# S5 scan and multi-query attention on one core: two shift passes, scan sums in PSUM, matmuls in column parts, and a replanned order

## The chip, the cores and the metric

The kernel runs on one core of a Trainium2 chip. The metric is device time in microseconds of one execution, from the first to the last instruction of the core. The core's engines are TensorE (PE; its weight loads are listed as PEld), VectorE (DVE), ScalarE (ACT), GpSimd (POOL) and SyncE (SP), which issues most transfers. They run side by side and wait for each other with semaphores.

## The reference

Two independent layers, both over 2048 positions of 640 features, whose outputs are put side by side (2048 x 1280, bfloat16).

```
# A: diagonal state-space layer, 640 complex states
Lam_bar = exp(dt * Lam);  Bu = x @ B_bar.T
h[t] = Lam_bar * h[t-1] + Bu[t]                 # over 2048 positions
yA = 2 * real(h @ C.T) + x * Dskip
# B: attention, 32 query heads of 20, one key head and one value head
q = (x @ wq) in 32 heads;  k = x @ wk;  v = x @ wv
p = softmax(q k^T * 20**-0.5)                   # 32 heads x 2048 x 2048
yB = (p @ v, heads side by side) @ wo
```

## The kernel before, in words

**Attention.** Queries are cut into 4 blocks of 512 and heads into 8 groups of 4, which gives 32 groups; each has 4 heads x 16 key blocks of 128. A *tile* is one head's scores of 128 keys x 512 queries: 2048 tiles in all. A score matmul takes only 32 or 64 rows of PE's array (`fill_op`), so that two to four run side by side. The result goes to one of two score buffers in PSUM, R0 (three banks) and R1 (two banks), or for one tile to a bank B0 or B1, or to R0's third bank ("lent", key R0c).

The exponential of a tile is taken in one of two ways. *On ACT* (`ex_op`, line 1263): one activation over the two or three tiles of R0 or R1, written to P. *On DVE*: `dx_op` (line 1269) adds an offset to the scores and writes them as 16-bit integers, whose bits are read as bfloat16; that is a piecewise linear 2^x. To even out its error, three copies shifted by 33, 65 and 95 parts of 128 of an octave are made of it by `sh_op` (line 1274: subtract, clamp at zero), for up to three tiles at once, and each copy is weighted in the value matrix VP. Such a tile so needs four PV matmuls where one of ACT needs one. All PV matmuls (`pv_op`) take 32 of the array's columns each, one head per 32 columns, four side by side, and add up in the PSUM bank PV. At a group's end DVE copies PV out (`raw_op`, line 1307).

**Scan.** The complex recurrence is turned by a per-state angle into two real scans with a real decay. For each of 20 units (4 time blocks x 5 state blocks of 128): `scan_in` computes Bu's two parts on PE in B0 or B1, and DVE multiplies each with cosine and sine into tm0 to tm3 (line 901); `scan_unit` forms the two sums tm0 + tm3 and tm2 - tm1 on POOL, in four pieces each, into the buffer uh (line 917); DVE scans each (line 928) into hh; POOL multiplies back with cosine and sine (tm4 to tm7) and adds up to W (line 917 too). `y_tile` multiplies W with C on PE and DVE copies the result out (line 962).

**Background.** Other matmuls, of the full 128 x 128 array: scan inputs, y tiles, query projections (`qd_block`), output projections (`proj_ops`), and `zero` matmuls that only keep PE streaming. Each takes a bank B0 or B1 from its first matmul (`lock`) until DVE has copied the result (`free`).

**Order.** No engine chooses its order while it runs. While the program is built, `main` simulates the engines with a table of durations (`Plan.add`, `mm_t`, `dve_t`, `act_t`), at each step takes the candidate that could begin first, with biases, and appends it to its engine's list. `Plan.add` also books 0.106 us for PE when the kind of matmul changes, and the time slots in which a fast DVE pass and POOL would meet (`slot`). `vary` draws the biases anew for each of 64 turns from a number in SEEDS. `want_d` decides whether the next tile goes to DVE: up to QUOTA = 16 of 64 per group, when a bank is free and DVE's backlog is short. A PE operation is put off behind the next fill if it would end later than `t_fill[1]`, the time at which the R buffer is free plus a drawn allowance (`after`).

All instructions of PE are issued from one line (421).

Of the kernel before, what the change touches and what calls it, by code (L numbers as in the profile page):

```python
# [20 lines left out]
class Plan:  # L21
# [12 lines left out]
    PRE = dict(dve=0.135, pool=0.05)  # L34

    def __init__(self, nc):
# [12 lines left out]
        self.run = 0  # L49
        self.port = deque([(-1.0, 0.0)], maxlen=48)  # L50
# [159 lines left out]
def mm_t(n, cold=1.0):  # L210
    return n / 2400.0 * cold + 0.003
# [32 lines left out]
class _Kernel:  # L244
# [5 lines left out]
    SHIFTS = (0, 33, 65, 95)  # L250
# [14 lines left out]
    SEEDS = (19006, 20002, 21006, 22006, 23001, 24003, 25001, 26002, 27008, 28003, 0, 30006, 31008, 32005, 33006,  # L265
# [11 lines left out]

    def calibration(self):
# [3 lines left out]
        for i in range(n):  # L282
            for sh in self.SHIFTS:
                f = (i / n - sh / 128.0) % 1.0
                tot += 0.25 * (1.0 + f) * 2.0 ** -f
# [8 lines left out]
    def alloc(self):  # L294
# [68 lines left out]
        self.sb("uh", [128, 2, 512], BF16)  # L363
# [47 lines left out]

    def mms(self, lst, reads, writes, accum=False, kind="D", **k):

        occ = sum(mm_t(x[2].free_size()) / x[6] for x in lst)
# [15 lines left out]
    def setup(self):  # L430
# [102 lines left out]
        def copy(eng, tb):  # L533
            bt, off, key = banks[tb]
            for h in range(2):
                dst, src = K.KT[:, h, 512 * tb:512 * tb + 512], bt[:, off:off + 512]
                if eng == "act":
                    yield Op("act", lambda e, dst=dst, src=src, h=h: e.activation(  # L538
                        dst, src, ACT.Copy, scale=K.half[:, h:h + 1]), [key, "half"], [f"KT{h}_{tb}"], occ=act_t(512),
# [16 lines left out]
        for tb in range(2):  # L556
# [19 lines left out]
            *(Op("dve", lambda e, i=i, sh=sh: e.memset(K.VP[:, i, :, 20:21], 2.0 ** (sh / 128.0)), ["VP"], ["VP"], occ=dve_t(16))  # L576
              for i, sh in enumerate(self.SHIFTS)),
            *(Op("dve", lambda e, i=i, sh=sh: e.tensor_scalar(K.VP[:, i, :, 0:20], vps, 2.0 ** (sh / 128.0), None,
# [4 lines left out]
        for c in range(NC):  # L583
            pool(lambda e, c=c: e.tensor_copy(K.wqd[:, c, :].rearrange("p (d h) -> p d h", h=32),
                                              K.wq_raw[:, c, :].rearrange("p (h d) -> p d h", d=20)),
                 ["wq_raw"] + pk, [f"wqd{c}"], occ=1.6)
# [153 lines left out]
    def qt_block(self, qb, gg, hold=None, gate=None, done=None):  # L740
# [7 lines left out]
        def mm(c):  # L748
            return self.mms([self.m1(lambda: h.T[:, :], (K.wq1, K.wq0p)[gg == 0][:, c, :], K.xbT[:, c, 512 * qb:512 * qb + 512],
                                     c == 0, False)], ["ystage", f"xbT{c}"] if gg == 0 else ["wq1"] + xs, [None], accum=c > 0,  # L750
# [6 lines left out]
                     accum=True, hold=h),  # L757
# [4 lines left out]
    def qd_block(self, qb):  # L762
# [5 lines left out]
        for m in range(NC):  # L768
            h = Hold()
            for c in range(NC):  # L770
                ops.append(self.mms([self.m1(lambda h=h: h.T[:, :], K.wqd[:, c, 128 * m:128 * m + 128],
                                             K.xbT[:, c, 512 * qb:512 * qb + 512], c == 0, c == NC - 1)],
                                    [f"wqd{c}"] + xs, [None], accum=c > 0, lock=c == 0, gate=gate if c == 0 else None,
# [15 lines left out]
        for x in seq:  # L789
# [5 lines left out]
            else:  # L795
                ops.append(self.mms([self.m1(lambda: h.T[0:32, :], K.Md[:, ng, :], K.Qab[:, ng % 2, :].bitcast(BF16),
                                             ng == 0, ng == NC - 1, (0, 0))], ["Md", f"Qa{ng % 2}"], [None], accum=ng > 0,
# [19 lines left out]
    def scan_ops(self):  # L817
# [34 lines left out]
        for c in range(NC):  # L852
            cr, ci = K.Craw[c][:, 0, :], K.Craw[c][:, 1, :]
            keys = [f"Craw{c}0", f"Craw{c}1", "sc"] + (["ostage0", "ostage1"] if c == 4 else ws)
            for (dst, x, y, gx, gy, op, nm) in ((K.CGre, cr, ci, GRE, GIM, ALU.subtract, "CGre"),
                                                (K.CGim, ci, cr, NGRE, NGIM, ALU.add, "CGim")):
                for i in range(0, 640, 128):
                    pool(lambda e, y=y, c=c, gy=gy, i=i: e.tensor_scalar(K.ctmp[:, i:i + 128], y[:, i:i + 128], sc[:, gy, c:c + 1],  # L858
                                                                         None, op0=ALU.mult), keys, [f"ct{i}"] + ct * (i == 0), 128)
# [4 lines left out]
        for b in range(4):  # L864
            for c in range(NC):
                self.scan_in(sa, mk(sa, "dve"), b, c)
                self.scan_unit(mk(su, "dve"), mk(su, "pool"), mk(sr, "pool"), b, c)
# [21 lines left out]
    def scan_in(self, ops, dve, b, c):  # L889
# [4 lines left out]
        for k, (nm, BT) in enumerate((("BTre", K.BTre), ("BTim", K.BTim))):  # L894
            h = Hold()
            for cd in range(NC):
                ops.append(self.mms([self.m1(lambda h=h: h.T[:, :], BT[:, cd, 128 * c:128 * c + 128],
                                             K.xaT[:, b % 2, cd, :], cd == 0, cd == NC - 1)],
                                    [f"{nm}{i}" for i in range(NC)] + xs, [None], accum=cd > 0, lock=cd == 0,
# [7 lines left out]
    def scan_unit(self, dve, pool, back, b, c):  # L907
# [16 lines left out]
        after = lambda: prog["r"] >= u  # L924
        dec = bass.AP(tensor=K.sc, offset=self.RDEC * NC + c, ap=[[24 * NC, 128], [0, 512]])
        for ri in range(2):
            ini = 0.0 if b == 0 else K.hini[:, ri, c:c + 1]
            dve(lambda e, ri=ri, ini=ini: e.tensor_tensor_scan(K.hh[:, ri, :], dec, K.uh[:, ri, :], ini, ALU.mult,  # L928
                                                               ALU.add), ["sc", *(f"uh{ri}{h}" for h in self.PIECES), "hini"], [f"hh{ri}"],
                1100,  # L930
                gate=after, done=(lambda: prog.update(s=u + 1)) if ri else None)
# [11 lines left out]
    def y_tile(self, ops, dve, b, q):  # L943
# [3 lines left out]
        for h, (o0, o1, ds) in enumerate(((0, 384, (0, 1, 2)), (384, 640, (3, 4)))):  # L947
# [10 lines left out]
            for i in range(0, len(lst), self.YMM):  # L958
                ops.append(self.mms(lst[i:i + self.YMM], self.w_keys + ["CGre", "CGim", "DiagD"]
                                    + [f"xaT{b % 2}_{c}" for c in range(NC)], [None], accum=i > 0, lock=i == 0,  # L960
# [56 lines left out]
    def norm_last(self, g):  # L1017
# [4 lines left out]
                                 t == 0, t == 3) for t in range(4)], ["E1", f"OTr{sl}"], [None], lock=True, hold=h0)]  # L1022
# [16 lines left out]
    def proj_ops(self, qb, part=False):  # L1039
# [4 lines left out]
        for ts in ((2, 3) if part else range(4)):  # L1044
# [3 lines left out]
            for h in range(2):  # L1048
# [4 lines left out]
                for i in range(0, len(lst), self.PMM):  # L1053
                    ops.append(self.mms(lst[i:i + self.PMM], ots + wo, [None], accum=i > 0, lock=i == 0, hold=hd,
# [13 lines left out]
    def last_ops(self, gates, normed):  # L1068
# [6 lines left out]
        def mm(ts, k, begin):  # L1075
            if k < NC:
                src, rd, ok = K.OTd[:, k, :], [f"OTd{k}{self.PIECES[ts]}"], lambda: self.NQB - 1 in self.dense
            else:
# [3 lines left out]
                            rd + self.wo_keys, keys[ts], accum=not begin, gate=lambda: gates[ts]() and ok())  # L1082
# [448 lines left out]
```

## Time and profile before

| | us |
|---|---|
| median of 3 runs | 768.98 (768.0 to 770.19) |
| profiled execution: span | 768.6 |
| ACT busy | 752.5 |
| DVE busy | 708.3 |
| PE covered by matmuls | 704.8 |
| POOL busy | 446.0 |
| mean granted TensorE clock | 0.989 |

A row of the groups of instructions has: line, engine, operation, output<-input by the program's names, their shapes, count, then busy us and the mean length of one in ns, then the idle us of the engine just before them and what ended most of it. Busy time counts overlaps once. Two neighbours on DVE or ACT overlap in the record, since the next begins while the last one's result is still being written; a mean length is therefore more than the step from one to the next. A row of a tile has minimum, median and maximum in ns, the first and last start, and its forms. A row of the timeline has the start, the length and the instruction, with neighbours of one kind merged. A row of the waits has who waited, for whom, us in total, how often, and the longest. A window's row has the busy time of PE, PEld, DVE, ACT and POOL, each with its count, then the granted clock, the share of the DMA engines, and GB/s.

### The profile page before, as it was taken

Reading aid. Unit: us, or ns where it says so; the run is one execution under the profiler, and the core shown is the slowest. Engines: PE = TensorE matmul, PEld = TensorE weight load, DVE = VectorE, ACT = ScalarE, POOL = GpSimd, SP = SyncE. Lnnn points to the kernel's source line nnn. Section 1 sums busy time; section 2 is a strip of 40 time slices with the busy share of each in tenths; the row PEclk is TensorE's granted clock in tenths of the full one; section 3 lists DMA queues with packets and bytes.
Section 4 is the critical chain, followed back from the end, with each engine's and each line's share of the span. In section 5 each row is a group of like instructions: output and inputs, shape, how many; then the busy total and the mean of one; then the engine's idle time right before and its main releaser. Section 6 shows DMA issues by size and latency. Waiting matters only on the chain.

```text
span 768.6 us, 16664 instructions
## 1 busy us (share of the span) xinstructions
PE 704.8 (92%) x6538; PEld 213.4 (28%) x6538; DVE 708.3 (92%) x1236; ACT 752.5 (98%) x710; POOL 446.0 (58%) x867
## 2 busy tenths in 40 slices
PE   5799988888889999998889999988889999889998
PEld 2222222222222333322223323322223332223333
DVE  5599999999998999999997999999999789999986
ACT  8999999999999999999999999999999999999995
POOL 5612354579989931088997300199986469990040
PEclk9899999899999999999999999999999999999999
DMA  9366301000021100220002100040000201000020
GB/s 186 57 143 134 74 16 49 8 24 14 3 51 30 42 8 27 56 60 15 15 9 67 42 23 9 23 93 10 15 15 28 66 33 34 14 15 17 18 61 35
DMA packets 61179, 31.50 MB, mean 41 GB/s; under 512 B 41510, under 2 KB 61102, under 8 KB 61102
## 3 DMA queue, kind: packets, MB, share of 16 engines
q1 hardware_dynamic: 59606, 30.14, 15.9%
q8 instruction: 52, 0.85, 0.5%
q10 hardware_dynamic: 1496, 0.30, 0.2%
q14 instruction: 25, 0.20, 0.1%
HBM read 9.21 MB, written 12.69 MB: 28 GB/s over the span
## 4 chain that ended last, share of the span: by engine, by line
ACT 74%; PE 15%; DVE 9%; POOL 1%; DMA 1%; issue 1%; ACTq 0%; DVEq 0%; POOLq 0%
ACT P L1263 72%; PE R L421 5%; PE PV L421 5%; PE B L421 4%; DVE Pd L1274 4%; DVE Pd L1269 3%; DVE hh L928 1%; DVE tm L901 1%; POOL tm L858 1%; DMA WO<-in_B_wk_dram 1%; ACT cs L691 1%; ACT Pd L690 0%; ACT KT L538 0%; DVE CGre L860 0%; ACT L503 0%
## 5 line engine op out<-in xcount | busy, mean ns | idle before, releaser
L1263 ACT ACTIVATE P<-R 128x1024 bf16<-128x1024 f32 (+1 forms) x677 | 733.1, 1354 | 4.3 <-PE R L421 1.8
L421 PE MATMUL R<-QT,KT 32*128 32x512 bf16 (+1 forms) x1685 | 266.9, 389 | 48.6 <-ACT P L1263 37.1
L1269 DVE TENSOR_SCALAR Pd<-B 128x512 int16<-128x512 f32 x363 | 245.5, 682 | 19.4 <-PE B L421 17.0
L1274 DVE TENSOR_SCALAR Pd<-Pd 128x1536 int16<-128x1536 int16 (+2 forms) x513 | 260.2, 541 | 0.4
L421 PE MATMUL PV<-Pd,VP 128*32 128x512 bf16 x1744 | 256.9, 386 | 2.0 <-DVE OTr L1307 1.0
L421 PE MATMUL PV<-P,VP 128*32 128x512 bf16 x1612 | 253.3, 389 | 0.7 <-DVE OTr L1307 0.6
L917 POOL TENSOR_TENSOR tm<-hh,cs 128x128 bf16<-128x128 f32 x320 | 163.9, 533 | 17.7 <-DVE hh L928 8.3
L421 PEld LDWEIGHTS R<-QT,KT 32*128 32x128 bf16 (+1 forms) x1685 | 66.1, 91 | 301.0 <-ACT P L1263 271.0
L421 PE MATMUL B<-QT,KT 32*128 32x512 bf16 x363 | 141.0, 389 | 0.0
L917 POOL TENSOR_TENSOR uh<-tm 128x128 bf16<-128x128 bf16 x160 | 81.0, 527 | 97.6 <-DVE tm L901 93.7
L917 POOL TENSOR_TENSOR W<-tm 128x128 bf16<-128x128 bf16 x160 | 93.5, 608 | 49.4 <-PE B L421 45.3
L421 PEld LDWEIGHTS PV<-Pd,VP 128*32 128x32 bf16 x1744 | 60.1, 94 | 65.7 <-issue 40.5
L421 PEld LDWEIGHTS PV<-P,VP 128*32 128x32 bf16 x1612 | 58.1, 94 | 58.8 <-issue 46.6
L1011 POOL TENSOR_TENSOR OTd<-OTd,rwide 128x128 bf16<-128x128 bf16 x80 | 33.2, 443 | 60.0 <-DMA OTd<-o_rows 58.2
L1269 DVE TENSOR_SCALAR Pd<-R 128x512 int16<-128x512 f32 x73 | 49.9, 683 | 3.0 <-PE R L421 2.4
L901 DVE TENSOR_TENSOR tm<-B,cs 128x1024 bf16<-128x1024 f32 x40 | 48.5, 1213 | 1.0 <-PE B L421 0.6
L858 POOL TENSOR_SCALAR tm<-W,sc 128x128 f32<-128x128 bf16 x40 | 32.3, 821 | 27.5 <-DVE CGre L860 15.9
L421 PE MATMUL B<-CGre,W 128*128 128x384 bf16 (+1 forms) x160 | 46.4, 305 | 0.0
L421 PE MATMUL B<-CGim,W 128*128 128x384 bf16 (+1 forms) x160 | 45.5, 299 | 0.0
L928 DVE TENSOR_TENSOR_SCAN hh<-sc,hini,uh 128x512 f32<-128x512 f32 x30 | 40.7, 1358 | 0.0
L421 PEld LDWEIGHTS B<-QT,KT 32*128 32x128 bf16 x363 | 32.9, 91 | 0.0
L421 PE MATMUL B<-xaT,BTre 128*128 128x512 bf16 x100 | 30.1, 384 | 0.1
(149 smaller groups left out, 437.2 us busy)
## 6 DMA issues: line engine op xcount, KB each, us to landing
o_rows<-OTr SPq DMA_DIRECT2D x32, 128.0 KB, 1.7
QT<-q_rows SPq DMA_DIRECT2D x30, 128.0 KB, 2.2
q_rows<-Qd SPq DMA_DIRECT2D x16, 160.0 KB, 2.9
OTd<-o_rows SPq DMA_DIRECT2D x16, 160.0 KB, 3.4
out_dram<-ystage SPq DMA_DIRECT2D x16, 160.0 KB, 1.9
out_dram<-ostage SPq DMA_DIRECT2D x12, 160.0 KB, 1.8
P<-in_B_wq_dram SPq DMA_DIRECT2D x1, 800.0 KB, 5.6
WO<-in_B_wo_dram SPq DMA_DIRECT2D x4, 200.0 KB, 3.4
```

Of the source, the lines that this page charges most:

```text
L421: ins = e.matmul(o() if callable(o) else o, lhsT=l, rhs=r, start=st, stop=sp, skip_group_check=True, **kw)
L691: act(lambda e, c=c, b=b: e.activation(K.cs[:, c, :, :].rearrange("p i n -> p (i n)"), K.tri[:, 4 * b + 2:4 * b + 4, :].rearrange("p r n - ...
L858: pool(lambda e, y=y, c=c, gy=gy, i=i: e.tensor_scalar(K.ctmp[:, i:i + 128], y[:, i:i + 128], sc[:, gy, c:c + 1], None, op0=ALU.mult), key ...
L901: dve(lambda e, k=k, h=h: e.tensor_tensor(K.tm[:, 2 * k:2 * k + 2, :], bass.AP(tensor=K.BB, offset=512 * int(h.key[1]), ap=[[512 * self.BA ...
L917: put(lambda e, c0=c0, end=end: e.tensor_tensor(out[:, c0:end], a[:, c0:end], b[:, c0:end], op), reads, [writes + h], n, gate=None if i el ...
L928: dve(lambda e, ri=ri, ini=ini: e.tensor_tensor_scan(K.hh[:, ri, :], dec, K.uh[:, ri, :], ini, ALU.mult, ALU.add), ["sc", *(f"uh{ri}{h}" f ...
L1011: ops.append(Op("pool", lambda e, c=c, m=m: e.tensor_tensor(K.OTd[:, m, c], K.OTd[:, m, c], K.rwide[:, c], ALU.mult), rw + [f"OTe{dd}" for ...
L1263: return Op("act", lambda e: e.activation(dst, K.R[n % 2][:, 0:512 * size], ACT.Exp, scale=self.exp_scale), [f"R{n % 2}"] + ["R0c"] * (siz ...
L1269: return Op("dve", lambda e: e.tensor_scalar(K.Pd[:, 0, u, :], K.B[x][:, :], self.d_off, 0.0, op0=ALU.add, op1=ALU.max), [key], [f"Pd{u}_0 ...
L1274: return Op("dve", lambda e: e.tensor_scalar(K.Pd[:, i, a:b, :], K.Pd[:, 0, a:b, :], float(self.SHIFTS[i]), 0.0, op0=ALU.subtract, op1=ALU ...
```

## The change

1. *Shift passes.* The shifts become 0, 32, 64, 96. `sh_op` takes a pair (i, n) from PASSES = ((1, 1), (2, 2)): the first pass makes copy 1 from copy 0, the second makes copies 2 and 3 from copies 0 and 1 in one instruction over two separate slabs. The weights in VP are rounded to a bfloat16 value. A group closes at `self.shift` tiles, drawn as 3, 3 or 4.
2. *Scan sums.* uh is gone. PE adds tm0 and tm3 in a bank B with two matmuls against the identity; tm2 - tm1 with the identity and its negative (`nident`, one POOL operation in setup). The scan reads the bank and frees it.
3. *Column parts.* Background matmuls have kind C; `mms` cuts each of kind C or zero into four of 32 columns (`cols`), issued one after another.
4. *Planner.* A change of tiling costs 0.1 us, and only between the forms QK, D and C (PV, zero and C are one form); the exponentials overlap by AHEAD, TRAIL and GRAIN; some durations are new; a fill's due time is counted back from the end of the exponentials that are planned ahead of it; the draws have new ranges and new parameters (among them the quota of 16, 18 or 22), and SEEDS is new.

```diff
-    SHIFTS = (0, 33, 65, 95)
+    SHIFTS = (0, 32, 64, 96)
+    PASSES = ((1, 1), (2, 2))
...
+    @staticmethod
+    def form(kind):
+        return kind if kind in ("QK", "D", None) else "C"
...
         if eng == "pe":
-            occ += 0.106 if kind != self.pe_kind else 0.01
+            occ += 0.1 if self.form(kind) != self.form(self.pe_kind) else 0.01
...
         if eng == "dve":
-            lat += self.DRAIN
-        if kind == "fast" or eng == "pool":
+            lat = self.DRAIN
+        if kind == "ex":
+            start = max(start, self.exp_end - self.AHEAD)
+            self.exp_end = max(start + occ + self.TRAIL, self.exp_end + occ + self.GRAIN)
+            lat = self.exp_end - start - occ
...
+    def cols(lst):
+        def part(o, j):
+            return (lambda: o()[32 * j:32 * j + 32]) if callable(o) else o[32 * j:32 * j + 32]
+        return [(part(o, j), l[:, 32 * j:32 * j + 32], r, st, sp, (0, 32 * j), 4)
+                for o, l, r, st, sp, tp, _ in lst for j in range(4)]
...
     def mms(self, lst, reads, writes, accum=False, kind="D", **k):
+        if kind in ("C", "zero") and lst[0][5] is None:
+            lst = self.cols(lst)
...
-        pieces(pool, K.uh[:, 0, :], tm[0], tm[3], ALU.add, ["tm0", "tm3"], "uh0",
-               gate=lambda: prog["a"] > u and prog["s"] >= u)
-        pieces(pool, K.uh[:, 1, :], tm[2], tm[1], ALU.subtract, ["tm1", "tm2"], "uh1",
-               done=lambda: prog.update(u=u + 1))
...
+        for ri, (x, y, sign) in enumerate(((0, 3, K.ident), (2, 1, K.nident))):
             ini = 0.0 if b == 0 else K.hini[:, ri, c:c + 1]
-            dve(lambda e, ri=ri, ini=ini: e.tensor_tensor_scan(K.hh[:, ri, :], dec, K.uh[:, ri, :], ini, ALU.mult,
+            h = Hold()
+            unit.append(self.mms([self.m1(lambda h=h: h.T[:, :], w[:, :], tm[k], i == 0, i == 1)
+                                  for i, (w, k) in enumerate(((K.ident, x), (sign, y)))],
+                                 ["ident", "nident", f"tm{x}", f"tm{y}"], [None], kind="C", lock=True, gate=gate, hold=h,
+                                 done=(lambda: prog.update(u=u + 1)) if ri else None))
+            dve(lambda e, ri=ri, ini=ini, h=h: e.tensor_tensor_scan(K.hh[:, ri, :], dec, h.T[:, :], ini, ALU.mult, ALU.add),
+                ["sc", None, "hini"], [f"hh{ri}"], 1100, hold=h, free=True,
...
-        self.backlog = r.choice((2.5, 3.0, 3.5, 4.0, 5.0))
+        self.backlog = r.choice((2.0, 2.5, 3.0))
...
-        self.after = r.choice((0.1, 0.15, 0.2)), r.choice((0.35, 0.4, 0.5))
+        self.after = (r.choice((-0.1, 0.0, 0.1)),) * 2
...
+        self.alone, self.eager = r.choice((0.0, 0.1, 0.2, 0.4)), r.choice((0.1, 0.2, 0.3))
+        self.patience, self.shift = r.choice((0.0, 0.15, 0.3, 0.6)), r.choice((3, 3, 4))
+        self.quota, self.pvb = r.choice((16, 18, 22)), r.choice(((0.0, 0.6), (0.0, 0.3), (0.05, 0.5), (0.1, 0.6)))
...
-        def sh_op(us, i):
+        def sh_op(us, ps):
             a, b = us[0][0], us[-1][0] + 1
...
+            i, n = ps
+            return Op("dve", lambda e: e.tensor_scalar(K.Pd[:, i:i + n, a:b, :].rearrange("p s u n -> p s (u n)"),
+                                                       K.Pd[:, 0:n, a:b, :].rearrange("p s u n -> p s (u n)"),
+                                                       float(self.SHIFTS[i]), 0.0, op0=ALU.subtract, op1=ALU.max),
...
+                      occ=dve_t(512 * n * (b - a), 4), kind="fast")
...
-                    t_fill = (t_fill, t_fill + self.after[n % 2])
+                    due_t = p.exp_end + sum(act_t(512 * len(x)) + p.GRAIN for _, x in tiles) - p.TRAIL - 0.45
+                    t_fill = (t_fill, max(t_fill + 0.05, due_t - self.after[n % 2]))
```

More of the change, by code (lines that the diff above doesn't have):

```diff
@@ L34 @@
     PRE = dict(dve=0.135, pool=0.05)
+    AHEAD, TRAIL, GRAIN = 0.42, 0.115, 0.0133
     def __init__(self, nc):
@@ L959, in y_tile @@
                 ops.append(self.mms(lst[i:i + self.YMM], self.w_keys + ["CGre", "CGim", "DiagD"]
-                                    + [f"xaT{b % 2}_{c}" for c in range(NC)], [None], accum=i > 0, lock=i == 0,
+                                    + [f"xaT{b % 2}_{c}" for c in range(NC)], [None], accum=i > 0, kind="C", lock=i == 0,
                                     gate=gate if i == 0 else None, hold=hd))
@@ L1224, in d_group @@
                 g += 1
-            return g if g < NG and g in qt_done and sum(dcount[g]) < self.QUOTA else None
+            return g if g < NG and g in qt_done and sum(dcount[g]) < self.quota else None
         def t_left():
@@ L1317, in main @@
             if half and not any(x[1][0] == half[0][1][0] for x in dunits) and taken[half[0][1][0]] > self.DLAST:
-                shifts.extend((tuple(half), i) for i in range(1, 4))
+                shifts.extend((tuple(half), x) for x in self.PASSES)
                 half.clear()
@@ L1344, in main @@
                         if d:
-                            offer("fill", fill_op(n, [], d, bank(None)), 0.2, arg=([], d, bank(None)))
+                            offer("fill", fill_op(n, [], d, bank(None)), self.alone, arg=([], d, bank(None)))
             full = bool(tiles) and tile_left.get(tiles[0][0] - self.PTILES, 0) > 0
@@ L1362, in main @@
                 if n > 0 and n < 99:
-                    offer("pv", pv_op(g), 0.1 if n > self.few or whole or p.pe_kind == "PV" else 0.6)
+                    offer("pv", pv_op(g), self.pvb[not (n > self.few or whole or p.form(p.pe_kind) == "C")])
                 elif n == 0 and (full or dunit_left.get(cur["d"] - self.DUNITS, 0)) and any(items[g]):
@@ L1410, in main @@
             if kind == "flush":
-                shifts.extend((tuple(half), i) for i in range(1, 4))
+                shifts.extend((tuple(half), x) for x in self.PASSES)
                 half.clear()
@@ L1460, in main @@
                 if half and (u == 0 or half[0][1][0] != g):
-                    shifts.extend((tuple(half), i) for i in range(1, 4))
+                    shifts.extend((tuple(half), x) for x in self.PASSES)
                     half.clear()
```

89 lines of the change are left out of this document (47 added, 42 removed), and 8 rows, old and new, of the table SEEDS.

## The prediction

> **What bounds the kernel now.** I read the page's busy shares first, then the groups of instructions by form, then the stage between setup and tail as one window, then the waits.
>
> ```profile
> span 768.6 us, 16664 instructions
> ...
> PE 704.8 (92%) x6538; PEld 213.4 (28%) x6538; DVE 708.3 (92%) x1236; ACT 752.5 (98%) x710; POOL 446.0 (58%) x867
> ```
>
> ```profile
> 21.68 2.37 ACT L1263 ACTIVATE P<-R 128x1536 bf16<-128x1536 f32 x2
> ...
> 628.31 130.73 ACT L1263 ACTIVATE P<-R 128x1536 bf16<-128x1536 f32 x119 [0.28 <-PE B L421]
> 763.92 0.70 ACT L1101 ACTIVATE W<-R 128x640 bf16<-128x640 f32 x1 [4.88 <-PE R L421]
> ```
>
> ```profile
> 60.00:740.00 680.00, 632.52 (x5900) 188.18 (x5899) 645.59 (x1102) 677.27 (x627) 411.93 (x783) 0.99 0.13 33
> ```
>
> Three stretches: setup until the first exponential at 21.7, exponentials until 628.31 + 130.73 = 759.0, and a tail of 9.6 us. Between 60 and 740 ACT idles 2.7 us of 680, DVE 34.4, and PE is covered 93%. So in the middle the time is ACT's work, and it shrinks only if ACT gets less to do, or if setup and tail shrink.
>
> ```profile
> L1263 ACT ACTIVATE P<-R 128x1024 bf16<-128x1024 f32 (+1 forms) x677 | 733.1, 1354 | 4.3 <-PE R L421 1.8
> ```
>
> ```profile
> L1263 ACT ACTIVATE P<-R 128x1024 bf16<-128x1024 f32 x419 | 457.8, 1189 | 1.1 <-PE R L421 0.7 <-PE B L421 0.2
> L1263 ACT ACTIVATE P<-R 128x1536 bf16<-128x1536 f32 x258 | 418.3, 1621 | 3.2 <-PE R L421 1.2 <-PE B L421 1.1 <-PE PV L421 0.6
> ...
> L1269 DVE TENSOR_SCALAR Pd<-B 128x512 int16<-128x512 f32 x363 | 245.5, 682 | 19.4 <-PE B L421 17.0
> ...
> L1269 DVE TENSOR_SCALAR Pd<-R 128x512 int16<-128x512 f32 x73 | 49.9, 683 | 3.0 <-PE R L421 2.4
> ```
>
> The work is 2048 score tiles (32 head groups x 4 x 16). ACT takes 419 x 2 + 258 x 3 = 1612 of them, DVE 363 + 73 = 436. Together, overlaps counted once, they take 733.1 us (the page's row), so one tile costs ACT 0.455 us. **The exchange rate** between the two engines is what the change turns on: DVE time that is freed becomes time saved only by way of more tiles on DVE.
>
> **The change, part by part.** *Two shift passes instead of three.*
>
> ```profile
> L1274 DVE TENSOR_SCALAR Pd<-Pd x513: 272/550/840, 36.2 to 758.3; 128x1536 int16<-128x1536 int16 x118, 128x1024 int16<-128x1024 int16 x29, 128x512 int16<-128x512 int16 x24
> ```
>
> ```profile
> L1274 DVE TENSOR_SCALAR Pd<-Pd 128x1536 int16<-128x1536 int16 x354 | 205.5, 608 | 0.2
> ...
> L1274 DVE TENSOR_SCALAR Pd<-Pd 128x1024 int16<-128x1024 int16 x87 | 35.8, 450 | 0.2
> ...
> L1274 DVE TENSOR_SCALAR Pd<-Pd 128x512 int16<-128x512 int16 x72 | 20.9, 323 | 0.1
> ```
>
> ```profile
> 307.35 1.28 DVE L1269 TENSOR_SCALAR Pd<-B 128x512 int16<-128x512 f32 x2
> ...
> 310.08 1.96 DVE L1274 TENSOR_SCALAR Pd<-Pd 128x1536 int16<-128x1536 int16 x4
> ```
>
> There are 118 + 29 + 24 = 171 groups with three passes each. The elements stay the same (the second new pass does twice as many), so only the fixed part of 171 passes goes. Four passes of 1536 in 1.96 us follow each other at (1.96 - 0.08)/4 = 0.47 us, where 0.08 is what two neighbours overlap (two L1269 take 1.28, one takes 0.68, so they start 0.60 apart). The undisturbed lengths, 0.272 for one tile and 0.55 for three, give 0.139 a tile, so the fixed part of a 0.47 step is about 0.06: 171 x 0.06 = 10 us. By the means of the forms (323, 450, 608) it is 0.18 - 0.08 = 0.10, or 17 us, disturbances included. I take 10 and count the disturbances below.
>
> The second pass reads what the first wrote, which none of the old passes 2 and 3 did:
>
> ```profile
> 496.42 0.42 DVE L1274 TENSOR_SCALAR Pd<-Pd 128x1024 int16<-128x1024 int16 x1
> 496.75 0.68 DVE L1269 TENSOR_SCALAR Pd<-B 128x512 int16<-128x512 f32 x1
> 497.47 0.56 DVE L1274 TENSOR_SCALAR Pd<-Pd 128x1536 int16<-128x1536 int16 x1
> ```
>
> A pass that directly follows the L1269 that it reads starts 0.72 us after it instead of 0.60: 0.12 of waiting. At worst 171 x 0.12 = 20.5 us, at best nothing, when another DVE operation is put between; what waits behind it is DVE's whole queue. The old first pass had the same wait, and its groups show only 0.5 us of idle, so it is mostly covered; I take a loss of a third, 7.
>
> *Scan sums on PE.*
>
> ```profile
> L917 POOL TENSOR_TENSOR uh<-tm x160: 417/428/1295, 64.9 to 672.9; 128x128 bf16<-128x128 bf16 x160
> L928 DVE TENSOR_TENSOR_SCAN hh<-sc,hini,uh x30: 1267/1316/1546, 259.9 to 677.7; 128x512 f32<-128x512 f32 x30
> L928 DVE TENSOR_TENSOR_SCAN hh<-sc,uh x10: 1198/1258/1443, 72.6 to 234.1; 128x512 f32<-128x512 f32 x10
> ```
>
> ```profile
> L917 POOL TENSOR_TENSOR uh<-tm 128x128 bf16<-128x128 bf16 x160 | 81.0, 527 | 97.6 <-DVE tm L901 93.7
> ...
> L860 DVE SCALAR_TENSOR_TENSOR CGre<-W,sc,tm 128x640 bf16<-128x640 bf16 x4 | 3.5, 876 | 0.5 <-POOL tm L858 0.5
> ...
> L1104 DVE TENSOR_TENSOR W<-B,wqd 128x640 bf16<-128x640 f32 x1 | 0.8, 825 | 0.0
> ```
>
> POOL loses 81.0 of 446.0 us; it bounds nothing, so that alone is worth zero. But the spread of L1274 (0.55 median undisturbed, 0.608 mean) is 354 x 0.058 + some 5 for the small forms = 26 us of DVE waiting, which I put down to POOL's accesses. With 18% of POOL gone that is 5 us; with a third fewer passes too, up to 12; at least 0. The scans themselves fall from their medians towards their minima if they too stop colliding, 40 x 0.05 = 2 us (0 to 3.6 by the means): an operand in PSUM is no dearer in the two 640-wide rows, 825 against 876. The Trainium skill ("GPSIMD Engine Reference", section "Key points") says that GpSimd shares its SBUF interfaces with VectorE and contends with VectorE instructions in a two-port mode or with two SBUF inputs; the old scan has two SBUF inputs and the new one has one, so by that page the scans' gain would be the whole 3.6.
>
> PE gains 40 sums of two 512-column rounds, and each holds one of two banks until its scan ends, some 0.6 + 1.3 us, 76 us of 2 x 680. A sum waits at the head of PE's queue for DVE's L901; behind it stand the next fill and, for that, ACT.
>
> *Column parts.*
>
> ```profile
> 300.59 0.39 PE L421 MATMUL R<-QT,KT 32*128 32x512 bf16 x2
> ...
> 300.91 0.40 PE L421 MATMUL PV<-Pd,VP 128*32 128x512 bf16 x3
> ...
> 301.14 0.38 PE L421 MATMUL PV<-Pd,VP 128*32 128x512 bf16 x2
> ...
> 761.74 0.41 PE L421 MATMUL B<-ident,rden 128*32 128x128 bf16 x16
> ```
>
> ```profile
> PEld R L421 <- ACT P L1263: 271.0, 598, 1.5
> ...
> PEld B L421 <- issue: 59.9, 242, 0.4
> ...
> DVE Pd L1269 <- PE B L421: 17.0, 58, 0.7
> ```
>
> ```profile
> L421 PE MATMUL B<-xaT,BTre 128*128 128x512 bf16 x100 | 30.1, 384 | 0.1
> ...
> L421 PEld LDWEIGHTS PV<-P,VP 128*32 128x32 bf16 x1612 | 58.1, 94 | 58.8 <-issue 46.6
> ...
> L421 PEld LDWEIGHTS B<-xaT,BTre 128*128 128x128 bf16 x100 | 6.7, 97 | 13.7 <-issue 10.8 <-DVE Pd L1269 0.9 <-DVE Pd L1274 0.4
> ```
>
> A round of four PV matmuls takes 0.22 us (300.91 to 301.14), a fill followed by PV 0.32: a change of tiling costs PE 0.10. 242 loads for B waited so; those that came from PV and not from a fill are saved, with as many on the way back: 0 to 24 us, I take 15. The 40 sums cost 40 x 2 x 0.22 = 17. PE's work stays about even, hidden behind its 271 us of waiting for ACT. What it wins is order: sums, projections and PV share one tiling and can be mixed. The four parts are paid in instructions (roughly 900 matmuls become 3600), which run at the same rate: 16 small ones of 128 columns, four abreast, end 0.41 after the first began, 0.05 a round beside the 0.2 that a single one takes. The Trainium skill ("TensorEngine Tiling (Array Packing)", section "Restrictions and Gotchas") speaks against this part: column tiling switches Fast Weight Load off. By it each of the four loads could cost what one costs now; the trace has 94 ns for a 32-column load beside 97 for a 128-column one, but four of them vanish behind every 0.22 us round.
>
> *Planner.* DVE idles 34.4 us between 60 and 740, 17.0 + 2.4 of the whole run behind a late PE. The quota of DVE tiles per group rises from 16 to 16, 18 or 22, fills need not go first any more, and durations change. I take 15 of this idle time as filled; bounds -10 (banks held by scans, fills crowding) and +25. Setup gets one short POOL operation, hidden behind 320 us of POOL idling; no DMA is added or moved. The tail saves some four changes of tiling, 0.4.
>
> **Sum.** DVE time freed F = 10 - 7 + 5 + 2 + 15 = 25 us; bounds 10 - 20.5 + 0 + 0 - 10 = -20 and 17 + 0 + 12 + 3.6 + 25 = 58 (the 17 counts some disturbance twice). A further tile costs DVE 0.60 + (0.47 + 0.87)/3 + 0.05 = 1.10 us. Moving n tiles shortens the run by 0.455 n, in which DVE loses as much: F = 1.10 n + 0.455 n, n = F/1.555. F = 25 gives 16 tiles and 7.3 us; the bounds give +6 and -17. With the tail, 768.6 - 7.7 = 760.9 for a profiled execution; the median of the runs, 768.98, stands 0.4 above the span: **761**, between 756 and 767 for this case.
>
> **Rivals.**
> *All of it is found:* F near the upper bound, pass waits covered, DVE idle near 10: 768.98 - 17 = 752. For it: only 0.5 us of idle before old passes. Against: PE is 93% covered in the middle, and needs four PV matmuls for each DVE tile against one. 0.20.
> *No change:* the second pass waits every time and the banks eat the rest, F = 0: 769. For it: two banks only, one wait more. 0.09.
> *Slower, fills too late:* the new due time of a fill is counted back from ACT's end instead of forward from the bank's release. ACT's 677 exponentials idle 4.3 us in all today, since fills go as soon as ACT releases R (the 271 us). If each fill came 0.023 us too late on average, that is 677 x 0.023 = 15.6, and 769 - 7.7 + 15.6 = 777. It decides above 7.7/677 = 11 ns per exponential. Against it: the fill needs 0.32 of the 0.9 us that an exponential of two tiles lasts. 0.16.
> *Slower, column parts load-bound:* if four loads ran one after another, 4 x 0.097 = 0.39 against 0.22 per 512-column round: 0.17 x some 500 wide rounds = 85 us more PE, more than its free 47 between 60 and 740; 769 + 85 - 47 - 8 = 799. The rounds of PV speak against it; what the Trainium skill's "TensorEngine Tiling (Array Packing)" says of Fast Weight Load is the rule behind it. 0.05.
> *The double pass runs at half rate* on its two separate slabs, so the change does not do what it says: 1536 x 2 at twice 0.139 a tile is 0.8 us more, 171 x 0.8 = 137; F = 25 - 137, +33: 802. The trace has no slabbed pass. 0.04.
>
> **How the numbers follow.** The forecast has 0.46. A change under 0.3% (2.3 us) can't be told from none here. Faster: 0.46 + 0.20 = 0.66; same 0.09; slower 0.16 + 0.05 + 0.04 = 0.25. The range 748 to 777 takes in the forecast, the better case, no change and most of the late fills, and leaves out the two slow cases.
>
> **What would show it.** Right: some 342 passes, with forms of 1536 and 3072, the latter near 0.95 us; about 450 L1269; L928 near its minima; POOL near 365; idle before L1263 still under 8 us; no POOL uh; DVE idle between 60 and 740 near 20. Wrong: L1263 idle of 10 us or more behind PE R; a 3072 pass above 1.3 us; idle before L1274 of 10 us; L1269 at 436 or fewer; B loads waiting for "issue" as often as now.

## The result and the profile after

The kernel after takes 761.44 us (median of 4 runs, 759.82 to 762.26), the kernel before, beside it, 769.5 (768.0 to 770.19): a ratio of 0.9894, 95% interval 0.9876 to 0.9913. It is 8.1 us faster; 761 was forecast. The profiled execution has a span of 758.1 us against 768.6, 10.5 less, which is some 2 us more than the medians differ by.

The busy shares of the page, then the exponentials in the timeline of ACT (first and last row), then the window from 60 to 740 us, all of the kernel after:

```profile
span 758.1 us, 22782 instructions
...
PE 697.1 (92%) x9725; PEld 226.4 (30%) x9725; DVE 699.6 (92%) x1084; ACT 743.4 (98%) x705; POOL 347.5 (46%) x708
```

```profile
20.88 9.17 ACT L1295 ACTIVATE P<-R 128x1536 bf16<-128x1536 f32 x8
...
695.87 53.49 ACT L1295 ACTIVATE P<-R 128x1536 bf16<-128x1536 f32 x48 [0.26 <-PE B L448]
```

```profile
60.00:740.00 680.00, 633.01 (x8902) 202.52 (x8898) 643.76 (x975) 677.84 (x631) 321.34 (x643) 0.99 0.13 35
```

The exponentials now run from 20.88 to 695.87 + 53.49 = 749.4, against 21.7 to 759.0: 8.8 us of the 10.5 lie in that stretch, 0.8 in a setup that ended earlier, 0.9 in the tail (8.7 us against 9.6). Inside the stretch ACT is as full as before (2.2 us idle of 680, before 2.7). So it must have had less to do.

The groups by form of the kernel after (line numbers have moved: 1263 is 1295, 1269 is 1301, 1274 is 1307, 928 is 957, 421 is 448):

```profile
L1295 ACT ACTIVATE P<-R 128x1024 bf16<-128x1024 f32 x421 | 452.5, 1174 | 0.2
L1295 ACT ACTIVATE P<-R 128x1536 bf16<-128x1536 f32 x250 | 400.4, 1602 | 4.1 <-PE B L448 2.2 <-PE R L448 1.6
...
L1301 DVE TENSOR_SCALAR Pd<-B 128x512 int16<-128x512 f32 x374 | 251.8, 682 | 22.1 <-PE B L448 19.6
...
L1307 DVE TENSOR_SCALAR Pd<-Pd 128x3072 int16<-128x3072 int16 x84 | 81.8, 974 | 0.5
...
L1301 DVE TENSOR_SCALAR Pd<-R 128x512 int16<-128x512 f32 x81 | 55.2, 682 | 2.7 <-PE R L448 1.9
...
L1307 DVE TENSOR_SCALAR Pd<-Pd 128x1536 int16<-128x1536 int16 x84 | 48.0, 572 | 0.5
...
L957 DVE TENSOR_TENSOR_SCAN hh<-sc,hini,B 128x512 f32<-128x512 f32 x30 | 37.6, 1268 | 0.6 <-PE B L448 0.3
...
L957 DVE TENSOR_TENSOR_SCAN hh<-sc,B 128x512 f32<-128x512 f32 x10 | 11.8, 1209 | 0.2
```

DVE takes 374 + 81 = 455 tiles where it took 436: 19 more. The page's two rows for exponentials and passes of the kernel after:

```profile
L1295 ACT ACTIVATE P<-R 128x1024 bf16<-128x1024 f32 (+2 forms) x672 | 724.2, 1333 | 4.3 <-PE B L448 2.2
...
L1307 DVE TENSOR_SCALAR Pd<-Pd 128x1536 int16<-128x1536 int16 (+3 forms) x342 | 241.0, 711 | 2.5
```

ACT's exponentials fell from 733.1 to 724.2, 8.9 us, which is 0.47 a tile. The passes fell from 260.2 us for 436 tiles to 241.0 for 455, from 0.597 to 0.530 us a tile: at the old price 455 tiles would have cost 271.6, so 30.6 us of DVE were freed there. The scans fell from 40.7 + 12.9 to 37.6 + 11.8, 4.2 us. DVE's idle time between 60 and 740 did not shrink: 680 - 643.76 = 36.2, before 34.4. Freed time is then 30.6 + 4.2 - 1.8 = 33 us, and 33/1.555 is 21 tiles; 19 were moved. Counted by DVE's whole busy time it is a little less: that fell by 8.7 us (708.3 to 699.6) with 19 tiles more on it, 1.10 us each as forecast, which makes 29.6 freed, less 1.8 of idle 28 us, or 18 tiles.

### The profile page after: what moved, and what is told of

Same layout as the page of the kernel before. It is cut to its first block, busy times and chain, and to the rows that moved or that the text cites. A ratio compares the mean times of both kernels' runs of the same rounds, so it can differ in the third digit from the quotient of the medians.

```text
span 758.1 us, 22782 instructions
## 1 busy us (share of the span) xinstructions
PE 697.1 (92%) x9725; PEld 226.4 (30%) x9725; DVE 699.6 (92%) x1084; ACT 743.4 (98%) x705; POOL 347.5 (46%) x708
## 4 chain that ended last, share of the span: by engine, by line
ACT 87%; PE 9%; DVE 3%; DMA 1%; issue 0%; ACTq 0%
ACT P L1295 85%; PE R L448 3%; PE B L448 3%; PE PV L448 3%; DVE Pd L1301 1%; DVE Pd L1307 1%; ACT cs L719 1%; DMA WO<-in_B_wk_dram 1%; ACT Pd L718 0%; ACT KT L565 0%; ACT L530 0%; DVE hh L957 0%; DVE tm L929 0%; ACT WO L507 0%; ACTq L421 0%
## 5 line engine op out<-in xcount | busy, mean ns | idle before, releaser
L1295 ACT ACTIVATE P<-R 128x1024 bf16<-128x1024 f32 (+2 forms) x672 | 724.2, 1333 | 4.3 <-PE B L448 2.2
L1301 DVE TENSOR_SCALAR Pd<-B 128x512 int16<-128x512 f32 x374 | 251.8, 682 | 22.1 <-PE B L448 19.6
L448 PE MATMUL PV<-P,VP 128*32 128x512 bf16 x1593 | 261.5, 386 | 0.2
L1307 DVE TENSOR_SCALAR Pd<-Pd 128x1536 int16<-128x1536 int16 (+3 forms) x342 | 241.0, 711 | 2.5
L945 POOL TENSOR_TENSOR W<-tm 128x128 bf16<-128x128 bf16 x160 | 76.0, 498 | 124.9 <-PE B L448 121.0
L448 PE MATMUL B<-CGre,W 128*32 128x384 bf16 (+1 forms) x640 | 48.5, 304 | 0.5 <-DVE Pd L1301 0.5
L448 PE MATMUL B<-CGim,W 128*32 128x384 bf16 (+1 forms) x640 | 47.8, 299 | 0.0
L886 POOL TENSOR_SCALAR tm<-W,sc 128x128 f32<-128x128 bf16 x40 | 32.7, 831 | 31.7 <-DVE CGre L888 14.9
L961 POOL COPY hst<-hh 128x2 f32<-128x2 f32 x15 | 5.9, 394 | 72.4 <-DVE hh L957 72.2
L957 DVE TENSOR_TENSOR_SCAN hh<-sc,hini,B 128x512 f32<-128x512 f32 x30 | 37.6, 1268 | 0.6 <-PE B L448 0.3
L448 PE MATMUL B<-xaT,BTre 128*32 128x512 bf16 x400 | 30.8, 383 | 0.7 <-DVE hh L957 0.3
```

What stands on the lines that cost most here:

```text
L448: ins = e.matmul(o() if callable(o) else o, lhsT=l, rhs=r, start=st, stop=sp, skip_group_check=True, **kw)
L945: put(lambda e, c0=c0, end=end: e.tensor_tensor(out[:, c0:end], a[:, c0:end], b[:, c0:end], op), reads, [writes + h], n, gate=None if i el ...
L957: dve(lambda e, ri=ri, ini=ini, h=h: e.tensor_tensor_scan(K.hh[:, ri, :], dec, h.T[:, :], ini, ALU.mult, ALU.add), ["sc", None, "hini"], [ ...
L961: pool(lambda e: e.tensor_copy(K.hst[:, :, c:c + 1], K.hh[:, :, 511:512]), ["hh0", "hh1"], ["hst"], 40)
L1295: return Op("act", lambda e: e.activation(dst, K.R[n % 2][:, 0:512 * size], ACT.Exp, scale=self.exp_scale), [f"R{n % 2}"] + ["R0c"] * (siz ...
L1301: return Op("dve", lambda e: e.tensor_scalar(K.Pd[:, 0, u, :], K.B[x][:, :], self.d_off, 0.0, op0=ALU.add, op1=ALU.max), [key], [f"Pd{u}_0 ...
```

## The experiments

The plan of this kernel depends on 64 drawn numbers, and a part cannot be undone without the whole order changing with it. So the first question was how much the numbers do by themselves. In the first four runs SEEDS alone is replaced, in the kernel after and in the kernel before.

```diff
-    SEEDS = (31, 1860, 2783, 3329, ...
+    SEEDS = (500, 1500, 2500, 3500, ...
```

after_draws_a, the kernel after with 500, 1500 and so on:

> The kernel after, with its 64 draws replaced by the fixed numbers 500, 1500, 2500 and so on; nothing else differs. Theory S (the structure gives the gain: cheaper shift passes and fewer collisions with POOL put more tiles on DVE, whatever the draws): at most 3 us above the kernel after, 758 to 764, still below the kernel before, with 450 or more tiles on DVE. Rival D (the draws give it): 772 to 785, with 440 or fewer tiles on DVE, and ACT or DVE idle where it is not now.

after_draws_b, the kernel after with 501, 1501 and so on:

> The same with the numbers 501, 1501, 2501 and so on. Theory S: within 2 us of the other set of fixed draws and below the kernel before. Rival D: 770 to 785, several us away from the other set.

before_draws_a and before_draws_b, the kernel before with the same numbers:

> The kernel before with the draws 500, 1500, 2500 and so on. Theory S: slower than the kernel after with the same draws by about the 8 us that the change measured. Rival D: its draws too were worth much, 785 to 795; then the change is worth 10 us or more at equal, unchosen draws, and a good part of the gain may be the planner's durations.

> The kernel before with the draws 501, 1501, 2501 and so on. Theory S: about 8 us above the kernel after with the same draws. Rival D: 783 to 798.

| run | us | ratio to the kernel before (95%) | tiles on DVE |
|---|---|---|---|
| after_draws_a | 781.06 | 1.0139 (1.0062 to 1.0217) | 417 |
| after_draws_b | 777.17 | 1.0084 (1.0057 to 1.0111) | 422 |
| before_draws_a | 789.47 | 1.0249 (1.0187 to 1.0310) | 422 |
| before_draws_b | 794.30 | 1.0311 (1.0231 to 1.0392) | 423 |

Theory S falls as it was put: with unchosen draws the kernel after is slower than the kernel before with its own ones. Rival D had the four times right. Unchosen draws cost the kernel after 16 and 20 us, and the kernel before 20 and 25. With the same unchosen numbers (which each planner turns into biases of its own) the kernel after leads by 8 and 17 us, the first as theory S had it, the second as rival D, though DVE has no more tiles in it than in the other. Where its lead lies there, the groups by form show; here the tiles on DVE of after_draws_a:

```profile
L1301 DVE TENSOR_SCALAR Pd<-B 128x512 int16<-128x512 f32 x344 | 233.9, 685 | 36.7 <-PE B L448 33.5
```

and the exponentials of before_draws_b, then of after_draws_b:

```profile
L1263 ACT ACTIVATE P<-R 128x1024 bf16<-128x1024 f32 x418 | 450.5, 1156 | 14.9 <-PE PV L421 11.9 <-PE R L421 2.0 <-PE B L421 0.7
L1263 ACT ACTIVATE P<-R 128x1536 bf16<-128x1536 f32 x263 | 417.0, 1585 | 7.6 <-PE B L421 4.7 <-PE R L421 1.5 <-PE PV L421 0.8
```

```profile
L1295 ACT ACTIVATE P<-R 128x1024 bf16<-128x1024 f32 x410 | 446.0, 1158 | 2.3 <-PE R L448 1.3 <-PE PV L448 0.8
L1295 ACT ACTIVATE P<-R 128x1536 bf16<-128x1536 f32 x268 | 427.2, 1594 | 2.7 <-PE R L448 1.6 <-PE B L448 0.9
```

With a bad draw DVE waits longer for PE (33.5 us in after_draws_a, 19.6 with the kernel's own draws), and more tiles are left to ACT. In the kernel before ACT itself idles too: 14.9 + 7.6 us before its exponentials, where after_draws_b has 2.3 + 2.7. That is 17.5 us more, the whole lead of the second pair; for the first pair it is 15.3 against 7.8, 7.5 of its 8.4. So at unchosen draws the lead lies in ACT's idle time and not in the tiles.

For the parts, draws were therefore chosen alike for every structure: turn by turn, 41 numbers were tried for one turn, each was planned on for three turns (in the last third to the end of the plan), and the one was kept under which ACT's and DVE's remaining work was least. Four structures got draws in this way:

```diff
 chosen_undo_passes
-    PASSES = ((1, 1), (2, 2))
+    PASSES = ((1, 1), (2, 1), (3, 1))
 chosen_undo_sums
-            unit.append(self.mms([self.m1(lambda h=h: h.T[:, :], w[:, :], tm[k], i == 0, i == 1)
...
+        pieces(pool, K.uh[:, 0, :], tm[0], tm[3], ALU.add, ["tm0", "tm3"], "uh0",
+               gate=lambda: prog["a"] > u and prog["s"] >= u)
+        pieces(pool, K.uh[:, 1, :], tm[2], tm[1], ALU.subtract, ["tm1", "tm2"], "uh1",
...
 chosen_undo_cols
-        return kind if kind in ("QK", "D", None) else "C"
+        return kind if kind in ("QK", "PV", None) else "D"
...
-        if kind in ("C", "zero") and lst[0][5] is None:
-            lst = self.cols(lst)
...
```

> The kernel after with draws chosen anew: turn by turn, the best of 41 by how far ACT and DVE have come three turns later in the planner's own table. The three kernels beside it get draws by the same procedure, so that a part can be undone without the draws of another structure. All theories: 759 to 766, 450 to 458 tiles on DVE; the other three are measured against it.

> Three shift passes per group again (shifts 32, 64, 96, each made from the unshifted copy), draws chosen by the same procedure. Theory P (the fixed part of a pass and its collisions with POOL are what frees DVE): 5 to 8 us above chosen_after, 12 to 20 tiles fewer on DVE, the passes at 0.59 to 0.60 us a tile instead of 0.53. Rival (the passes' cost lies mostly in their elements, and DVE would have been freed anyway): within 2 us.

> The scan sums on POOL again in buffer uh, scans from SBUF, draws chosen by the same procedure. Theory C (POOL's 81 us of sums collide with the passes and scans): the 1536 pass back from 0.57 to 0.60 us or more, the scan back to 1.33, DVE loses some 15 us, 4 us above chosen_after. Rival (the banks held by the sums and PE's extra rounds cost as much as the collisions): within 1.5 us, or faster.

> Background and keep-warm matmuls whole again, 128 x 128, with the change of tiling booked for each switch to and from them; draws chosen by the same procedure. Theory (the column parts give PE freedom only, and PE is not what binds): 0 to 3 us above chosen_after, with more idle on DVE behind a late PE. Rival (a late PE is what starves DVE, so that column parts are the main gain): 6 us or more above it, 10 tiles fewer on DVE.

To these came a second chosen set of the first two, the three parts undone together, and the kernel before with draws chosen in the same way:

> The kernel after with a second set of draws chosen by the same procedure from other candidates; it measures how far two chosen sets lie apart. If chosen sets agree: 762 to 765. Rival (what the undone parts showed is the luck of a set): 767 or more, or 759 or less.

> Three shift passes with a second chosen set. Theory P: 766 to 770, some 10 tiles fewer on DVE than chosen_after_2. Rival (luck of a set): within 2 us of chosen_after_2.

> The new planner with all three structural parts undone (three passes, sums on POOL, whole matmuls), draws chosen by the same procedure. Theory (the parts add up): 4.6 + 0.9 + 1.5 = 7 us above chosen_after, 770 to 772, some 430 tiles on DVE. Rival (the planner's durations give most of the gain): 763 to 767.

> The kernel before, old planner and old structure, draws chosen by the same procedure instead of its own. Theory (the planner's durations are worth nothing when draws are chosen alike): 768 to 773, as chosen_planner_only, ACT's idle before the exponentials 5 us or less. Rival (the old table promises what the chip doesn't keep, so that choosing by it is worth less): 776 to 784, with 10 us or more of ACT idle behind PE.

| run | us | ratio to the kernel before (95%) | tiles on DVE | passes, us a tile |
|---|---|---|---|---|
| chosen_after | 763.28 | 0.9912 (0.9889 to 0.9934) | 446 | 0.540 |
| chosen_after_2 | 762.85 | 0.9907 (0.9889 to 0.9926) | 446 | 0.544 |
| chosen_undo_passes | 767.83 | 0.9984 (0.9959 to 1.0009) | 436 | 0.575 |
| chosen_undo_passes_2 | 768.62 | 0.9986 (0.9968 to 1.0004) | 439 | 0.580 |
| chosen_undo_sums | 764.16 | 0.9934 (0.9911 to 0.9957) | 444 | 0.544 |
| chosen_undo_cols | 764.75 | 0.9935 (0.9914 to 0.9956) | 446 | 0.542 |
| chosen_planner_only | 776.79 | 1.0083 (1.0054 to 1.0111) | 431 | 0.600 |
| chosen_before | 782.10 | 1.0164 (1.0141 to 1.0187) | 427 | 0.614 |

The last column is the busy time of the page's pass row over the tiles. These are the rows of chosen_after, chosen_undo_passes and chosen_planner_only, one fence each:

```profile
L1307 DVE TENSOR_SCALAR Pd<-Pd 128x1536 int16<-128x1536 int16 (+3 forms) x352 | 241.0, 693 | 3.3
```

```profile
L1307 DVE TENSOR_SCALAR Pd<-Pd 128x1536 int16<-128x1536 int16 (+3 forms) x510 | 250.5, 527 | 1.4
```

```profile
L1304 DVE TENSOR_SCALAR Pd<-Pd 128x1536 int16<-128x1536 int16 (+3 forms) x495 | 258.4, 555 | 1.4
```

**Chosen sets agree.** Two sets for the kernel after lie 0.4 us apart, with the same 446 tiles (450 to 458 were expected); two for three passes lie 0.8 apart. The rival that a set is luck falls. Two pairs are few, so I read differences of some 3 us and more between chosen runs, and no smaller ones.

How long the passes are held up by POOL can be read from the traces: for each pass, its length over the median length of those passes of its form during which POOL ran nothing, summed over all passes. POOL's recorded spans are rough, so the counts are too.

| run | passes | of these with POOL running | held up, us in all |
|---|---|---|---|
| before | 513 | 279 | 25.8 |
| after | 342 | 145 | 9.5 |
| chosen_after | 352 | 148 | 11.6 |
| chosen_after_2 | 358 | 159 | 11.7 |
| chosen_undo_passes | 510 | 184 | 16.4 |
| chosen_undo_passes_2 | 534 | 197 | 17.8 |
| chosen_undo_sums | 332 | 202 | 15.8 |
| chosen_planner_only | 495 | 276 | 26.8 |
| chosen_before | 516 | 277 | 32.5 |

That it is POOL shows within one trace: in the kernel before, a pass of 1536 takes 550 ns on average when POOL runs nothing (135 of them) and 643 when it runs something (219).

**Passes.** Undoing them costs 4.6 us (first sets) and 5.8 (second), intervals apart both times, and 10 and 7 tiles. A tile's passes cost 0.575 and 0.580 us against 0.540 and 0.544: 0.036 x 446 = 16 us of DVE; 5 to 6 of these are time held up by POOL (16.4 and 17.8 against 11.6 and 11.7), and the other 10 are what is left for the fixed part of the third pass. Theory P had 5 to 8 us, which the first pair misses by 0.4 and the second meets; its 12 to 20 tiles and 0.59 us a tile were too much. Its rival, 2 us, falls.

**Sums.** Undoing them costs 0.9 us, and the two intervals overlap. The groups by form of chosen_undo_sums show what was given and taken:

```profile
L1306 DVE TENSOR_SCALAR Pd<-Pd 128x3072 int16<-128x3072 int16 x93 | 92.6, 996 | 1.0
L944 POOL TENSOR_TENSOR uh<-tm 128x128 bf16<-128x128 bf16 x160 | 88.0, 569 | 59.9 <-DVE tm L928 55.7
L1306 DVE TENSOR_SCALAR Pd<-Pd 128x1536 int16<-128x1536 int16 x93 | 56.3, 605 | 0.7
...
L955 DVE TENSOR_TENSOR_SCAN hh<-sc,hini,uh 128x512 f32<-128x512 f32 x30 | 41.3, 1378 | 0.0
...
L955 DVE TENSOR_TENSOR_SCAN hh<-sc,uh 128x512 f32<-128x512 f32 x10 | 12.7, 1281 | 0.0
```

The scans are back at 1378 and 1281 ns (chosen_after has the scans of the kernel after to within 3 ns), 4.3 us in all. The 1536 pass is at 605 ns, against 592 and 602 in the two chosen sets of the kernel after, which by itself can't be read; but 202 passes meet POOL instead of 148 and 159, and they are held up 4 us longer in all. These collisions are real, but they come to some 8 us of DVE and not 15. Theory C falls in its size, and its rival, within 1.5 us, is met: whether the sums on PE are worth anything in time can't be told here.

**Column parts.** Undoing them costs 1.5 us with the same number of tiles, inside 0 to 3. The waits of chosen_undo_cols, then of chosen_after:

```profile
PEld PV L446 <- issue: 103.8, 437, 0.4
...
PEld B L446 <- issue: 67.1, 273, 0.4
...
DVE Pd L1299 <- PE B L446: 16.9, 50, 1.3
```

```profile
PEld PV L448 <- issue: 82.0, 359, 0.4
...
PEld B L448 <- issue: 48.7, 204, 2.1
...
DVE Pd L1301 <- PE B L448: 20.3, 58, 1.9
```

and the last of these rows in chosen_after_2:

```profile
DVE Pd L1301 <- PE B L448: 13.0, 49, 1.0
```

The waits for issue, which the prediction put down to changes of tiling, are 147 fewer with column parts (437 + 273 against 359 + 204). But no effect on DVE's wait for a late B can be read: 16.9 us without column parts lies between the 20.3 and 13.0 of the two sets with them, though the theory expected more idle there. The freedom is there and hardly anything hangs on it; 1.5 us is too little to be told from none. The rival that a late PE starves DVE and that column parts are the main gain falls.

**Planner.** With all three parts undone the new planner takes 776.79, outside both of what was expected: the single undoings add to 4.6 + 0.9 + 1.5 = 7.0 us, together they cost 13.5. Part of that can be seen in the passes, which cost most when there are three of them and POOL has the sums (0.600 us a tile, against 0.578 with three passes and the sums on PE, and 0.544 with two passes and the sums on POOL): they are held up 15 us longer than in chosen_after, where the single undoings give 5 to 6 and 4. The profiled executions lie 9.8 apart (773.8 and 764.0): 15 tiles fewer on DVE are 6.8 us of it, and ACT idles 5.4 instead of 2.8 us before its exponentials. Another part goes with the granted TensorE clock: the run at 773.8 had 0.985, the other three, at 775.9 to 777.7, had 0.976 to 0.979, while all but one of the 14 runs of chosen_after and chosen_after_2 had 0.992 or 0.993. That the time goes with the clock shows in the kernel before, run beside it: 768.0 to 769.1 at 0.989 and more, 770.4 to 772.0 at 0.987 and less. Whether the low clock comes from the kernel was not tried. The kernel before with draws chosen in this way takes 782.10 (clock 0.974 to 0.980), in its rival's range, 5.3 more than the new planner on nearly the same structure (its shifts differ). The groups of chosen_before show the idle of ACT that the rival wanted, if not quite as much, 5.4 + 3.5 us:

```profile
L1263 ACT ACTIVATE P<-R 128x1024 bf16<-128x1024 f32 x435 | 466.7, 1173 | 5.4 <-PE PV L421 2.9 <-PE B L421 1.5 <-PE R L421 0.7
L1263 ACT ACTIVATE P<-R 128x1536 bf16<-128x1536 f32 x250 | 400.7, 1603 | 3.5 <-PE B L421 2.2 <-PE R L421 1.3
```

It also means that the draws the kernel before came with are 12.6 us better than those that this procedure finds for it, while for the kernel after the procedure comes within 1.4 to 1.8 us of its own draws. So with draws chosen by this one procedure the change is worth 19 us (782.10 against 763.28 and 762.85), some of which goes with the lower clock; 11 of them had already been won for the kernel before by its own draws. Why these are so good for it was not tried, and so it stays open how the measured 8 us divide between the parts and the planner; the passes alone, 4.6 and 5.8 us, are shown.

None of the runs beats the kernel after.

## Why the prediction was right

**Bound and exchange rate: right.** ACT stayed full, and the gain came as tiles moved to DVE: 19 against 16 forecast, 0.47 us of ACT for each against 0.455. The sum's result, F = 25 us, was measured as 33, and its rule F/1.555 gives 21 tiles for that (by DVE's whole busy time 28 us and 18 tiles).

**The terms inside F: mis-sized, and in opposite directions.** Three of them:

*The passes were put too low.* Fixed part 10, less 7 for the second pass waiting for the first, and 5 for fewer collisions: 8 together. The two rows show 30.6. By the runs with chosen draws, 16 of this go with the third pass itself (0.036 us a tile between chosen_after and chosen_undo_passes); some 10 with the sums leaving POOL while there were three passes (0.600 to 0.578 between chosen_planner_only and chosen_undo_passes, which differ in the column parts too); and the draws of the kernel after do 0.012 a tile better than the chosen ones, 5 us. By kind, the collisions were mis-sized: the time held up by POOL went from 25.8 us, as the prediction had it, to 9.5, so 16 vanished, over three fifths, where 5 was taken and 12 was the upper bound. They had been scaled by POOL's share alone; but the passes that meet POOL fell by nearly half (279 to 145), POOL's busy time by a fifth (446.0 to 347.5), and a pass that met it lost 64 ns instead of 92. The other 14 are what is left for the fixed part, more than the 10 that was taken and less than its bound of 17.

*The wait of the second pass was put too high.* Idle before the passes rose from 0.4 to 2.5 us, so 2 and not 7. The timeline of DVE in the kernel after has an example of how the planner fills it:

```profile
706.53 0.56 DVE L1307 TENSOR_SCALAR Pd<-Pd 128x1536 int16<-128x1536 int16 x1
707.01 1.46 DVE L1301 TENSOR_SCALAR Pd<-B 128x512 int16<-128x512 f32 x2
708.38 0.68 DVE L1343 CAST OTr<-PV 128x512 bf16<-128x512 f32 x1
708.98 0.95 DVE L1307 TENSOR_SCALAR Pd<-Pd 128x3072 int16<-128x3072 int16 x1
```

Between the first pass of a group (706.53) and the second (708.98) stand three other operations. If the passes are paired by form and order, 131 of the 171 second passes have at least one operation between.

*The idle that was to be filled was not.* I took 15 of DVE's 34.4 us, and named an idle near 20 as the sign; it is 36.2. DVE waits for a late PE as long as before (19.6 + 1.9 us against 17.0 + 2.4), with fewer changes of tiling, a quota that may be higher and freer fills. The argument went from PE's saved switches to an earlier B; chosen_undo_cols shows no sign of that step, since without the column parts this wait lies between those of the two sets with them.

The misses cancel for the most part (+23 for the passes with their wait, -17 for the idle, +2 for the scans), and so the median came out within 0.5 us; the profiled execution, the fastest of the four, gained 10.5 us where 7.7 was forecast. That is luck in the terms; the bound and the exchange rate are what held for these two kernels.

**Scans.** 2 was taken, 4.2 measured, all scans now near their old minima (1268 and 1209 against 1267 and 1198). By their lengths the scans gave 30 x 0.090 + 10 x 0.086 = 3.6 us, the prediction's upper figure. In the kernel before, a scan of the 30 takes 1381 ns when POOL runs over more than half of it (22 of them) and 1273 when it runs nothing (7); in the kernel after 1266 (16) and 1268 (11). The Trainium skill ("GPSIMD Engine Reference", section "Key points") names contention with GpSimd for VectorE instructions with two SBUF inputs, and the new scan has one. The trace agrees.

**Rivals.** *Fills too late:* idle before the exponentials is 4.3 us, as before; it did not happen. *Load-bound column parts:* the rows of the kernel after have a four-part matmul no longer than a whole one was:

```profile
L448 PE MATMUL B<-xaT,BTre 128*32 128x512 bf16 x400 | 30.8, 383 | 0.7 <-DVE hh L957 0.3 <-issue 0.2
```

400 parts cover 30.8 us where 100 whole ones covered 30.1. What the Trainium skill ("TensorEngine Tiling (Array Packing)", section "Restrictions and Gotchas") says of Fast Weight Load costs nothing that shows here. *Double pass at half rate:* 974 ns for 3072 elements, 0.95 forecast; it runs at the full rate over two slabs. *All found:* the passes gave as much as their upper bounds together (17 + 12), the idle did not. *No change:* excluded by the interval.

**Setup and tail.** 0.8 and 0.9 us were gained there against 0.4 forecast; both are single executions.

## What to carry to other kernels

Where two engines share the same work, find the exchange rate first (here 1.555 us of DVE for 0.455 us of time) and turn every saving into moved units; that held while the single terms did not. It holds only while the bounding engine stays full: with unchosen draws the kernel after led by 8 and 17 us without a tile more on DVE, because ACT idled less. Where the instructions of two engines hold each other up, count in the trace how many of them meet: that number may fall faster (here by nearly half) than the work of either engine, so don't scale by one side's share. Where an order is searched by draws, undo a part only together with draws chosen again by one procedure: the draws alone moved these kernels by 16 to 25 us, twice the change and more.

## What the runs showed of the hardware that was not expected

Cutting a 128 x 128 matmul into four column parts cost PE next to nothing (30.8 us for 400 parts, 30.1 for 100 whole ones). That the busy time of PE fell from 704.8 to 697.1 us, with 3187 more matmuls (9725 against 6538, the sums among them), is no measure of it, since `zero` matmuls fill PE's gaps. Their rows in the kernel before and after:

```profile
L421 PE MATMUL PV<-cs,VP 128*128 128x512 bf16 x72 | 25.7, 394 | 0.0
```

```profile
L448 PE MATMUL PV<-cs,VP 128*32 128x512 bf16 x212 | 18.2, 382 | 0.0
```

Without them PE is covered 683.4 us before and 683.9 after. Between chosen_undo_cols and chosen_after, where the column parts alone differ in structure, it is 701.0 and 689.2: with them PE was even covered 12 us less, and the time did not change by more than can be told.

A pass of 1536 elements that met POOL took 643 ns on average in the kernel before and 597 in the kernel after, against 550 and 551 beside an idle POOL. At a POOL share of 46% and with two passes 9.5 us of 26 were left; with other draws, chosen_after, it was 11.6 at 45%. So the order counts too, and not the share alone. A scan with one input in PSUM took as long beside a busy POOL as beside an idle one (1266 and 1268 ns), while one with both in SBUF lost 0.11 us (1381 and 1273).
